# Two row tiles of a matmul one sum apart, released by a GpSimd token, with paced loads

## The chip, the cores and the metric

The kernel runs on one core of one Trainium2 chip. The metric is device time in microseconds (us). Runs are compared within the same rounds on the same chip; all runs compared here are in the fast state (the single look at one kernel has no state of its own and is marked). "Span" is the time from the first to the last instruction of the one profiled execution, some 1.7 to 2 us less than device time.

## The reference, cut to what matters

```python
# x: (8, 4096, 192); weight: (8 heads, 7); w_in: (192, 2048); w_out: (2048, 192); all float32
w = softmax(weight)                                   # per head
x_pad = concat([zeros(6 rows), x])                    # causal, per batch row
out = einsum('hk,bskhg->bshg', w, windows(x_pad, 7))  # a 7-tap convolution down the sequence
h = out.reshape(32768, 192) @ w_in
g = maximum(0.01 * h, h)
return g @ w_out
```

So: a depthwise convolution, a matmul up to 2048 columns, a leaky rectifier, a matmul down to 192.

## The kernel before

Two batch rows are worked on at once, 512 positions of each in a block; 32 blocks. The data of a block goes through these stages:

- GpSimd issues six loads of x with a cast to bf16 (`load_x`); SyncE (SP) issues three transposing DMAs (`transpose_x`), which lay the channels on the partitions.
- VectorE (DVE) does the convolution: 3 pieces of 64 channels, 7 instructions each.
- TensorE (PE) does the first matmul with two 64-row tiles side by side; ScalarE (ACT) takes the product out of PSUM (the memory, divided into banks, that TensorE writes to) through the rectifier.
- TensorE does the second matmul, also with two 64-row tiles. A "sum" is one output tile of 128 rows: 16 matmuls of row tile 0 and 16 of row tile 1, added into the same PSUM bank.

The first five blocks are cut into halves (ten groups of 256 positions), so that work can start early. Each group is a number of steps: two units of the first matmul, then a batch of slots of the second. In a slot row tile 0 does one matmul, and row tile 1 another one, `LAG` slots behind. The program must keep the two row tiles from writing one bank at the same time (the prediction names the page of the Trainium skill that says so). So row tile 1 starts a sum only after row tile 0 has finished it, and the order is kept by a dependency on an instruction of another engine:

```python
    LAG = NFC + NFC // 2          # 24 slots; a sum has NFC = 16
...
    def mm1(grp, u):
        ...                                       # the matmuls of one unit
        act = nc.scalar.activation(out=g[blk][...], in_=ph..., func=Prelu, alpha=0.01)
        while unsealed:
            seal[unsealed.pop()] = act.ins.name   # the release of finished sums

    def mm2_one(rt, m, fc):
        ins = nc.tensor.matmul(...)
        if rt == 0 and fc == NFC - 1:
            unsealed.append(m)
        if rt == 1 and fc == 0:
            tc.add_manual_dep(ins.ins, seal[m], ..., reason="other row tile, same bank")
...
        for j in range(steps):
            for u in range(2 * j, 2 * j + 2):
                mm1(grp, u)
            for _ in range(quota):
                mm2_slot(slot)                    # stores an output tile after every second sum
                slot += 1
            if i == 1 and j == 1:
                nc.gpsimd.tensor_copy(out=pjunk, in_=g[0][...])   # a gate: x waits for the weights
                load_x(2)
            if i == 2 and j == 1:
                transpose_x(2)
            for job in ahead[per * j : per * (j + 1)]:
                job()                             # convolution of the next group, on VectorE
            if j == steps // 4 and last_half:
                load_x(blk + 3)
            if j == steps // 2 and last_half and blk > 0:
                transpose_x(blk + 2)
```

## Time and profile before

| | before |
|---|---|
| median of 3 runs | 697.73 us (697.35 to 700.79) |
| span of the profiled run | 696.7 us |
| busy: TensorE, VectorE, ScalarE, GpSimd | 99%, 78%, 74%, 20% |
| opening (10 half groups), until the first full group | 117.5 us |
| one full block in the steady part | 20.96 us |

Two things are to be read here. The busy shares are means over the kernel. And a timeline line has the columns: start in us, length in us, engine, line, operation, output and input, shape, count, and in brackets the idle time of the engine before it, with what ended that. The lines themselves stand in the prediction.

### The profile page before, as it was taken

To read this page: it belongs to the slowest core of one execution; us is meant where nothing else is said; L and a number is where in the kernel's file an instruction comes from. 1 tells how busy PE (TensorE), PEld (TensorE's weight loads), DVE (VectorE), ACT (ScalarE), POOL (GpSimd) and SP (SyncE) were. 2 spreads that over 40 slices of the span, in tenths; PEclk is the share of its full clock that TensorE was granted. 3 is DMA by queue.
4 is the path that set the end of the run, shared out by engine and by line. 5 is a ranking of instruction groups with operands and counts; after the bars stand their busy time and mean duration, and the time that the engine had idled before them with its cause. 6 is when DMAs were issued, how large, how long until landed. Compare 5 with 4: busy or idle time off the path is not lost.

```text
span 696.7 us, 26003 instructions
## 1 busy us (share of the span) xinstructions
PE 688.9 (99%) x11756; PEld 611.7 (88%) x11756; DVE 542.4 (78%) x1000; ACT 512.3 (74%) x576; POOL 142.2 (20%) x199
## 2 busy tenths in 40 slices
PE   8999999999999999999999999999999999999997
PEld 6899998678888888888888888888888888888887
DVE  6899999867777787777787777787777787777712
ACT  6788887977777777777777777777777777777770
POOL 4732221320222220222211222220222210000000
PEclk9999999999999999999999999999999999999999
DMA  9987563754556545556644556544566535122112
GB/s 172 110 106 84 83 88 68 83 77 80 73 67 92 81 70 81 74 67 93 81 67 85 67 74 92 80 73 74 73 75 86 87 66 73 56 52 58 47 36 70
DMA packets 184847, 54.39 MB, mean 78 GB/s; under 512 B 148384, under 2 KB 184736, under 8 KB 184736
## 3 DMA queue, kind: packets, MB, share of 16 engines
q0 software_dynamic: 98768, 14.17, 29.4%
q1 hardware_dynamic: 85968, 38.56, 23.0%
q8 instruction: 92, 1.51, 0.9%
q14 instruction: 19, 0.16, 0.1%
HBM read 29.88 MB, written 25.17 MB: 79 GB/s over the span
## 4 chain that ended last, share of the span: by engine, by line
PE 83%; DVE 12%; DMA 3%; issue 1%; POOL 0%; ACT 0%; POOLq 0%; ACTq 0%
PE po L377 43%; PE ph L357 40%; DVE yt L182 11%; DMA w_out<-in_moe_w_out_dram 2%; DVE yt L176 1%; DMA w_in<-in_moe_w_in_dram 1%; POOL sel L228 0%; ACT g L364 0%; DVE xt L157 0%; POOL sel L226 0%; DVE o_sb L416 0%; POOL ident masks.py:199 0%; PE ptr L143 0%; POOL ident masks.py:197 0%; POOLq masks.py:199 0%
## 5 line engine op out<-in xcount | busy, mean ns | idle before, releaser
L364 ACT ACTIVATE g<-ph 128x1024 bf16<-128x1024 f32 x512 | 496.4, 1021 | 162.9 <-PE ph L357 162.9
L182 DVE SCALAR_TENSOR_TENSOR yt<-xt,wk,yt 128x512 bf16<-128x512 bf16 (+1 forms) x648 | 442.6, 683 | 17.6
L377 PE MATMUL po<-w_out,g 64*128 64x192 bf16 (+1 forms) x8048 | 398.2, 243 | 0.7 <-DMA w_out<-in_moe_w_out_dram 0.7
L377 PEld LDWEIGHTS <-g 64*128 64x128 bf16 (+1 forms) x8048 | 372.5, 94 | 29.4 <-issue 1.1
L357 PE MATMUL ph<-yt,w_in 64*128 64x512 bf16 (+1 forms) x3552 | 392.2, 347 | 2.3 <-ACT g L364 0.9
L357 PEld LDWEIGHTS <-w_in 64*128 64x128 bf16 x3552 | 250.1, 94 | 47.0 <-issue 5.3
L79 POOL DMA_DIRECT2D x_bf<-in_x_dram x180 | 133.6, 777 | 420.0 <-DMA xt<-x_bf 420.0
L416 DVE COPY o_sb<-po 128x192 f32<-128x192 f32 x216 | 77.3, 358 | 127.2 <-PE po L377 124.8
L176 DVE TENSOR_SCALAR yt<-xt,wk 128x512 bf16<-128x512 bf16 (+1 forms) x108 | 36.8, 340 | 0.2
L416 ACT COPY o_sb<-po 128x192 f32<-128x192 f32 x40 | 13.1, 327 | 0.0
L201 PE MATMUL acc<-xt,diag 64*64 64x256 bf16 x84 | 6.6, 319 | 0.0
L201 PEld LDWEIGHTS <-diag 64*64 64x64 bf16 x84 | 5.1, 126 | 1.4 <-issue 0.6
L250 PE MATMUL warm<-zero 128*128 128x256 bf16 x18 | 4.3, 399 | 1.1 <-DVE junk L218 1.1
L238 POOL DMA_DIRECT2D w_in<-in_moe_w_in_dram x8 | 5.1, 644 | 0.0
L157 DVE COPY xt<-ptr 128x384 bf16<-128x384 bf16 x7 | 2.2, 354 | 2.4 <-PE ptr L143 2.4
L250 PEld LDWEIGHTS <-zero 128*128 128x128 bf16 x18 | 2.0, 131 | 2.2 <-DVE junk L218 1.1
L296 ACT ACTIVATE diag<-ident,wkl 128x64 bf16<-128x64 bf16 x14 | 3.6, 336 | 0.0
L128 DVE CAST x_bf<-x_nat 128x384 bf16<-128x384 f32 x5 | 2.4, 499 | 1.4 <-DMA x_nat<-in_x_dram 1.4
L461 POOL COPY pjunk<-g 1x1 bf16<-1x1 bf16 x1 | 0.2, 177 | 12.0 <-ACT g L364 12.0
L128 ACT CAST x_bf<-x_nat 128x384 bf16<-128x384 f32 x3 | 1.5, 506 | 1.5 <-DMA x_nat<-in_x_dram 1.5
L317 ACT ACTIVATE yt<-acc,rsum 128x256 bf16<-128x256 f32 x2 | 0.9, 473 | 2.2 <-PE acc L201 2.2
L255 ACT ACT_TABLE_LOAD x1 | 1.3, 1283 | 0.8 <-PEq L498 0.8
(29 smaller groups left out, 13.7 us busy)
## 6 DMA issues: line engine op xcount, KB each, us to landing
out_dram<-o_sb SPq DMA_DIRECT2D x128, 192.0 KB, 2.1
x_bf<-in_x_dram POOLq DMA_DIRECT2D x180, 64.0 KB, 3.2
x_nat<-in_x_dram SPq DMA_DIRECT2D x8, 192.0 KB, 4.8
w_in<-in_moe_w_in_dram POOLq DMA_DIRECT2D x8, 192.0 KB, 8.7
xt<-x_bf SPq DMA_TRANSPOSE x90, 2.5
w_out<-in_moe_w_out_dram POOLq DMA_DIRECT2D x1, 768.0 KB, 14.7
w<-in_weight_dram SPq DMA_DIRECT2D x1, 0.2 KB
```

The lines of the kernel that those rows point to most:

```text
L79: nc.gpsimd.dma_start(out=t[:, c, :, e, :], in_=src[2 * rp + e, :, :, c * CH : (c + 1) * CH],)
L128: copy(out=x_bf[q // 2][:, :, h * HS : (h + 1) * HS, e, :], in_=x_nat[q][:, e, :, :].rearrange("p s (c k) -> p c s k", c=NCH),)
L176: lambda s=src, d=dst, c=c: nc.vector.tensor_scalar_mul(d, s, wk[:, c, 0:1])
L182: lambda s=src, d=dst, c=c, k=k: nc.vector.scalar_tensor_tensor(out=d, in0=s, scalar=wk[:, c, k : k + 1], in1=d, op0=mybir.AluOpType.mult, ...
L201: lambda k=k, p=p, a=a, e=e, ps=ps: nc.tensor.matmul(out=acc[ps, :T], lhsT=diag[c][ps, p, k, :], rhs=xt[0][ps, c, a : a + T], start=(k == ...
L238: nc.gpsimd.dma_start(out=w_in[e * CH : (e + 1) * CH, :, fs], in_=moe_w_in[:, fs].rearrange("(c p) f -> p c f", p=CH),)
L250: nc.tensor.matmul(out=wa[:, 0, 0:HT], lhsT=zero[:, 0:128], rhs=zero, start=True, stop=True)
L296: act = nc.scalar.activation(out=diag[c][:, 1, k, :], in_=ident2, func=mybir.ActivationFunctionType.Copy, scale=wkl[:, c, k : k + 1],)
L357: nc.tensor.matmul(out=ph[:, e, i * T : (i + 1) * T], lhsT=w_in[ps, c, f * 128 : (f + 1) * 128], rhs=y[ps, c, t0 : t0 + T], start=(c == 0) ...
L364: act = nc.scalar.activation(out=g[blk][:, nf * u : nf * (u + 1), :, t0 : t0 + T], in_=ph.rearrange("p e (i t) -> p i e t", i=nf), func=my ...
L377: ins = nc.tensor.matmul(out=po[m], lhsT=g[b][ps, fc, e, s * 128 : (s + 1) * 128], rhs=w_out[ps, fc, :], start=(rt != 1 and fc == 0), stop ...
L416: copy(out=o_sb[:, n % 2, :], in_=po.pop(n))
```

## The change

Its intent: shorten the lag to one sum, so that the end has fewer slots in which only one row tile works. Row tile 1 then needs its release at the very start of a batch, and the release comes from GpSimd: a one-element memset that follows the first matmul of the next step. Since GpSimd takes its queue in order, its loads must not hold the token up, so they are issued one in a step (two in the half groups). Three lines of the driver, which place loads and transposes, moved along with it.

```diff
-    LAG = NFC + NFC // 2
+    LAG = NFC
...
+                    if unsealed:                      # inside mm1, after its first matmul
+                        token = nc.gpsimd.memset(ptoken, 0.0)
+                        tc.add_manual_dep(token.ins, ins.ins.name, ..., reason="row tile 0 has left its bank")
+                        while unsealed:
+                            seal[unsealed.pop()] = token.ins.name
-        while unsealed:
-            seal[unsealed.pop()] = act.ins.name
...
-            if i == 2 and j == 1:
+            if i == 3 and j == 0:
                 transpose_x(2)
...
-            if j == steps // 4 and last_half:
+            if j == 0 and last_half:
                 load_x(blk + 3)               # now only puts six loads on a list
-            if j == steps // 2 and last_half and blk > 0:
+            if loads:
+                loads.pop(0)()
+            if loads and T < ST:
+                loads.pop(0)()
+            if j == steps - 2 and last_half and blk > 0:
                 transpose_x(blk + 2)
```

More of the change, by code (lines that the diff above doesn't have):

```diff
@@ L68 @@
     x_nat, x_bf, xt = {}, {}, {}
+    loads = []
     def load_x(blk):
@@ L78, in load_x @@
             for e in range(2):
-                nc.gpsimd.dma_start(
-                    out=t[:, c, :, e, :],
-                    in_=src[2 * rp + e, :, :, c * CH : (c + 1) * CH],
+                loads.append(
+                    lambda c=c, e=e: nc.gpsimd.dma_start(
+                        out=t[:, c, :, e, :],
+                        in_=src[2 * rp + e, :, :, c * CH : (c + 1) * CH],
+                    )
                 )
@@ L356, in mm1 @@
                     ps = slice(e * CH, (e + 1) * CH)
-                    nc.tensor.matmul(
+                    ins = nc.tensor.matmul(
                         out=ph[:, e, i * T : (i + 1) * T],
@@ L363, in mm1 @@
                     )
-        act = nc.scalar.activation(
+                    if unsealed:
+                        token = nc.gpsimd.memset(ptoken, 0.0)
+                        tc.add_manual_dep(
+                            token.ins, ins.ins.name,
+                            mybir.DependencyInfo(
+                                mybir.DependencyClass.Sync, mybir.DependencyReason.DATA
+                            ),
+                            reason="row tile 0 has left its bank",
+                        )
+                        while unsealed:
+                            seal[unsealed.pop()] = token.ins.name
+        nc.scalar.activation(
             out=g[blk][:, nf * u : nf * (u + 1), :, t0 : t0 + T],
@@ L424 @@
     pjunk = const_pool.tile([1, 1], BF16)
+    ptoken = const_pool.tile([1, 1], FP32)
     slot, avail = 0, 0
```

## The prediction

> **What bounds the kernel now.** I read the page first, then the chain of work that ended last in order of time, the waits, and the timeline around the places where that chain leaves TensorE. The page's busy line and its chain by engine:
>
> ```profile
> PE 688.9 (99%) x11756; PEld 611.7 (88%) x11756; DVE 542.4 (78%) x1000; ACT 512.3 (74%) x576; POOL 142.2 (20%) x199
> ...
> PE 83%; DVE 12%; DMA 3%; issue 1%; POOL 0%; ACT 0%; POOLq 0%; ACTq 0%
> ```
>
> TensorE (PE) looks like the only bound, but 12% of the chain is VectorE (DVE). The chain in order of time shows where: from the first token block (28.3 us) until 118.9 us it runs through the convolution on VectorE, without a break, and only then goes over to TensorE. The windows of those 90.6 us and of the long steady part:
>
> ```profile
> 28.30:118.90 90.60, 89.86 (x1908) 89.45 (x1904) 85.19 (x180) 73.33 (x103) 25.57 (x35) 1.00 0.70 86
> 140.00:660.00 520.00, 520.00 (x8738) 458.58 (x8734) 411.25 (x720) 384.66 (x398) 93.56 (x126) 1.00 0.50 74
> ```
>
> (Columns: window, length, busy PE, weight loads, DVE, ACT, POOL, then clock, DMA share, GB/s.) So there are two regimes. In the steady part PE is busy 520.00 of 520 and DVE 79%: PE bounds. In the opening part, ten groups of 256 rows, both are near full, and DVE sets the time: the timeline shows it arriving late at the first full group.
>
> ```profile
> 114.25 4.69 DVE L182 SCALAR_TENSOR_TENSOR yt<-xt,wk,yt 128x512 bf16<-128x512 bf16 x6
> ...
> 118.99 1.04 PE L357 MATMUL ph<-yt,w_in 64*128 64x512 bf16 x8 [0.83 <-DVE yt L182]
> ```
>
> The last convolution piece ends at about 118.94, and PE, idle for 0.83 us, goes on at 118.99. Any delay of VectorE between 28.3 and 118.9 moves the end of the kernel one for one. The place in that stretch which the change touches, from the timeline:
>
> ```profile
> 39.04 0.38 SPq L419 DMA_DIRECT2D out_dram<-o_sb  x1
> 39.53 4.57 SPq L94 DMA_TRANSPOSE xt<-x_bf  x3
> ...
> 43.55 0.28 DVE L176 TENSOR_SCALAR yt<-xt,wk 128x256 bf16<-128x256 bf16 x1
> 43.87 1.49 PE L357 MATMUL ph<-yt,w_in 64*128 64x256 bf16 x24
> ...
> 54.39 1.49 PE L357 MATMUL ph<-yt,w_in 64*128 64x256 bf16 x24
> ```
>
> The three transposes of block 2 start on the SyncE queue (SP) at 39.53 and are in by 44.10; VectorE reads the first of them at 43.55, with no idle time before it. PE wants the product of that convolution at 54.39.
>
> **What the Trainium skill says.** "PSUM — Partial Sum Buffer", section "PSUM bank collisions raise a hardware error", says that different row tiles may not write one PSUM bank at once and that software must order them; that is why row tile 1 needs a release at all. The trace shows no cost of this order now: among PE's waits none is for the second matmul's release. "Perfetto Trace Analysis", section "Tensor Engine Instruction", calls ACT, DVE and GpSimd strict FIFO, so a GpSimd token waits behind a load placed ahead of it; in this trace GpSimd waited 420.0 us in all at its loads, which would be fatal for a token. "GPSIMD Engine Reference", section "Specifications", says that GpSimd shares SBUF interfaces with VectorE. The trace agrees in part: one TENSOR_SCALAR of 128x256 at 46.88 took 0.54 us beside GpSimd's load issues, against 0.28 elsewhere, while the SCALAR_TENSOR_TENSORs kept their 0.50. "TensorE: Matmul & The Clock Gate", part 1, says that PE drops to half clock after an idle window of about 3.4 us; the trace before has no such idle stretch after the start (clock 1.00 in all windows).
>
> **The change part by part.**
> *Lag 24 to 16 slots.* A slot is one matmul of each row tile; from the timeline 16 slots take 1.32 us, 0.0825 each, also where only one row tile works. The number of slots is a constant plus the lag, so 8 fall away: 8 x 0.0825 = 0.66 us saved, at the end, where before 8 slots follow the last group. Otherwise it removes no PE time, as PE waits for nothing here now.
>
> *The token.* 247 memsets of one element (counted in the built program's order). A token follows the first matmul of a step, so it may run some 0.3 to 0.5 us into the step; its reader is the second weight load of the step's batch, at 1.29 us (timeline: 12 matmuls from 399.83, batch from 401.12). A memset of this kind took 0.10 us at the start of the trace. About 0.6 us of slack is left, so cost 0, if GpSimd is free. That is what the loads one a step are for: a load issue is 777 ns (745 to 879), it stands just after a token, and the next token comes 2.61 us later; with two a step (in the opening part) 1.55 us. Since each load is now requested after the transposes it depends on are long done, the 420 us of waiting should vanish. Cost 0.
>
> *Copies of the output move to the end of a step.* In a full block VectorE's step is then: copy at batch end + 0.28, three pieces to +2.88 (timeline: copy at 404.67, pieces to 407.27), as long as a PE step, 2.61. The last three pieces of a block fall in its last step and end 0.27 us into the next block, where PE wants them after two pairs of matmuls, 2 x 0.213 = 0.43. That fits by about 0.1 us. I allow 0.3 us in all for small misses over 21 blocks.
>
> *Loads of block 3 ahead of block 2, transposes of block 2 later.* This I expect to be the real cost. In the built order block 3's loads are now requested first (step 0 of the second group), then block 2's, so the transposes of block 2 go from step 1 of the third group to step 0 of the fourth; on SP four output stores stand ahead of them, before two. SP takes its queue in order; it waited 92.0 us in all for ACT's copies. The fourth store needs sum 7, whose row tile 1 now ends with the batch of that very step. From the trace: that batch ends at 46.50 (45.18 + 1.32); the copy starts 0.2 later (in the tail, batch end 679.57, copy at 679.77) and takes 0.33: 47.03; the store's issue until the transposes took 0.49 before (39.04 to 39.53): transposes at 47.5; one takes 2.5 us to land (page, part 6): 50.0, with the semaphore 50.1. VectorE would have started at 43.55: **6.55 us late.** Nothing else stands in its queue that it could do in between. PE then stalls about 5 us at 54.4 (third convolution piece at 50.1 + 3 x 3.32 = 60.1), and the rest, some 1.5 us, at the first full group, since PE's group takes 10.52 us and VectorE's 9.97. Everything after is PE bound again, so 6.55 us reach the end.
>
> *Early loads.* Two loads of block 3 are issued before the gate that kept x off the DMA engines until the weights are in. If they delay w_out (landing at 23.95, on the chain), all shifts. They stand behind it in the same queue, so I take 0.1 us, at most 2 (each load estimated at 1.06 us of all 16 engines: 29.4% of 16 x 697 us over 98,768 packets is 33 ns, by 512 packets, by 1/16).
>
> Sum: 697.7 - 0.66 + 6.55 + 0.3 + 0.1 = **704.0 us.**
>
> **Rivals.** (a) The opening delay does not occur: the transposes go early enough, or VectorE has slack. For it: the author chose the place on purpose, and VectorE's share looks moderate (78%). Against: the store ahead in SP's queue, and a chain through VectorE with no gap. It would give 697.1 to 697.5. (b) The token becomes the bound: GpSimd sits in a load or is held by VectorE, and each batch starts late; 0.2 us at each of 247 would be 49 us, 0.03 us 7 us. Against: 0.6 us of slack, load issues of at most 0.88 us. (c) VectorE's later copies make each full block late, by 0.1 to 0.3 us: 21 x 0.2 = 4 us more, 708. For it: the margin of only 0.1 us. Against: the page's idle time of VectorE before copies, 124.8 us, says it mostly waits for PE. (d) The 5 us stall cools PE's clock. It would cost some 1.7 us of PE time, but the later wait at the first full group (about 2.3 us) would hide it: 0.
>
> **Range and chances.** The main term rests on four measured durations and an order in the queue, so it is good to perhaps 1 us if the mechanism holds (85%). (a) takes 8%, (c) and early loads stretch the top. Range 700.5 to 708.0. Two per cent is 14 us; slower than that needs (b) or (c) in full, 5%; faster by 2% has no source, 1%; same 94%.
>
> **What would show it right or wrong.** In the changed profile: the first transpose of block 2 at about 47.5 after the fourth store; an idle stretch of VectorE of about 6.5 us before a TENSOR_SCALAR near 50; PE waiting for yt about 5 us near 54.5 and about 2.3 us near 124; the steady window still with PE at 100%, steps of 2.61 us, no PE wait for GpSimd; GpSimd's waits at transposes gone; the tail shorter by 0.66. Wrong if the transposes start before 45, if PE's waits for VectorE add up to under 3 us, or if the steady part's block differs from 20.96 us by over 0.1.

## The result, and the profile after

The changed kernel takes 705.45 us (median of 5 runs, 704.17 to 708.96), the kernel before in the same rounds 698.27 us. The ratio is 1.0106, with a 95% interval of 1.0073 to 1.0139. (A ratio here is the mean time of one kernel's runs over that of the other's runs of the same rounds, so it is not quite the ratio of the medians.) It is slower, by less than two per cent. The span went from 696.7 to 703.4 us.

The page of the changed kernel, its busy line and its chain by engine:

```profile
PE 689.6 (98%) x11756; PEld 550.0 (78%) x11756; DVE 549.1 (78%) x1000; ACT 516.5 (73%) x576; POOL 163.8 (23%) x446
...
PE 93%; DMA 3%; DVE 1%; ACT 1%; POOL 0%; issue 0%; SPq 0%; POOLq 0%
```

TensorE is busy for the same time as before, within 0.7 us, in a span 6.7 us longer: it idles more. VectorE has all but left the chain that ends last. The timeline of the changed kernel where block 2 is transposed, that is, the place that the prediction showed of the kernel before:

```profile
46.95 0.37 SPq L433 DMA_DIRECT2D out_dram<-o_sb  x1
47.44 3.94 SPq L98 DMA_TRANSPOSE xt<-x_bf  x3
51.40 0.29 DVE L180 TENSOR_SCALAR yt<-xt,wk 128x256 bf16<-128x256 bf16 x1 [8.40 <-DMA xt<-x_bf]
...
54.87 0.11 PEld L361 LDWEIGHTS <-w_in 64*128 64x128 bf16 x3 [0.65 <-DVE yt L186]
54.87 0.28 PE L361 MATMUL ph<-yt,w_in 64*128 64x256 bf16 x2 [0.43 <-ACT o_sb L430]
...
58.19 0.40 PE L361 MATMUL ph<-yt,w_in 64*128 64x256 bf16 x2 [3.03 <-DVE yt L186]
...
61.51 2.32 PE L361 MATMUL ph<-yt,w_in 64*128 64x256 bf16 x20 [2.92 <-DVE yt L186]
63.59 2.79 PE L391 MATMUL po<-w_out,g 64*128 64x192 bf16 x32
```

The fourth output store is issued at 46.95, the transposes follow at 47.44, and VectorE, idle for 8.40 us, gets the first at 51.40 instead of 43.55. TensorE then waits three times for the convolution, 6.4 us in all. (The first of the three matmul lines names ScalarE's copy instead, but that copy was over at 54.86, within 0.05 us of the convolution piece, 51.73 + 3.09 = 54.82; the weight load of the same moment names the convolution.) The last line shows an after-effect: a batch of 32 matmuls took 2.79 us, where it takes 1.50 elsewhere. The windows of that place and of the steady part (columns as in the prediction; the clock is the third number from the end):

```profile
62.00:68.00 6.00, 6.00 (x78) 5.55 (x76) 5.61 (x13) 2.92 (x4) 0.09 (x1) 0.58 0.06 19
68.00:74.00 6.00, 6.00 (x136) 6.00 (x132) 5.61 (x14) 5.25 (x8) 0.18 (x2) 1.00 0.16 49
143.69:687.63 543.94, 543.94 (x9141) 416.95 (x9136) 425.14 (x734) 404.12 (x419) 120.53 (x346) 1.00 0.50 75
```

The granted clock was 0.58 in the 6 us from 62 on, and 1.00 in the next 6. The last window holds the 26 full blocks after the first; the same blocks took, in the kernel before:

```profile
135.19:680.23 545.04, 545.04 (x9141) 479.88 (x9137) 416.92 (x732) 404.08 (x419) 96.95 (x131) 1.00 0.49 73
```

545.04 - 543.94 = 1.10 us less, over 26 blocks 0.042 us each. With that the whole difference can be added up. The lines at the two ends, first of the kernel before, then of the changed one:

```profile
135.19 1.58 PE L357 MATMUL ph<-yt,w_in 64*128 64x512 bf16 x12
678.91 14.13 PE L377 MATMUL po<-w_out,g 64*128 64x192 bf16 x168
...
143.69 1.48 PE L361 MATMUL ph<-yt,w_in 64*128 64x512 bf16 x12
686.31 13.47 PE L391 MATMUL po<-w_out,g 64*128 64x192 bf16 x160
```

| term | before | after | difference, us |
|---|---|---|---|
| first matmul of the second full group | 135.19 | 143.69 | +8.50 |
| the 26 full blocks | 545.04 | 543.94 | -1.10 |
| the last batch and the matmuls after it: 168 in 14.13 us, then 160 in 13.47 | 14.13 | 13.47 | -0.66 |
| sum | | | +6.74 |

(The last batch, 1.32 us in both kernels, also belongs to the last full block, so the rows overlap by it; the differences do not change.) The spans differ by 6.7 us, so nothing is left over. The 8.50 us fall in two. The last convolution piece for the first full group ended at 118.94 before (114.25 + 4.69) and at 126.34 after (121.65 + 4.69 in its timeline), 7.40 later. The other 1.10 are TensorE's: it reached that group only at 127.06, and did not wait there at all:

```profile
121.65 4.69 DVE L186 SCALAR_TENSOR_TENSOR yt<-xt,wk,yt 128x512 bf16<-128x512 bf16 x6
...
127.06 1.47 PE L361 MATMUL ph<-yt,w_in 64*128 64x512 bf16 x12
```

GpSimd, in the waits, no longer stands at its loads (420.0 us before) but at its tokens, as intended:

```profile
POOL ptoken L370 <- PE ph L361: 453.3, 247, 13.5
```

And no wait of TensorE for the token appears among its waits.

### The profile page after: what moved, and what is told of

Read it like the earlier page. It is cut to its first block, busy times and chain, and to the rows that moved or that the text cites. A ratio compares the mean times of both kernels' runs of the same rounds, so it can differ in the third digit from the quotient of the medians.

```text
span 703.4 us, 26493 instructions
## 1 busy us (share of the span) xinstructions
PE 689.6 (98%) x11756; PEld 550.0 (78%) x11756; DVE 549.1 (78%) x1000; ACT 516.5 (73%) x576; POOL 163.8 (23%) x446
## 4 chain that ended last, share of the span: by engine, by line
PE 93%; DMA 3%; DVE 1%; ACT 1%; POOL 0%; issue 0%; SPq 0%; POOLq 0%
PE po L391 48%; PE ph L361 45%; DMA w_out<-in_moe_w_out_dram 2%; DVE yt L186 1%; ACT g L380 1%; DMA w_in<-in_moe_w_in_dram 1%; DMA xt<-x_bf 1%; POOL sel L232 0%; DVE yt L180 0%; SPq L433 0%; POOL sel L230 0%; DVE o_sb L430 0%; ACT o_sb L430 0%; POOL ident masks.py:199 0%; POOL ident masks.py:197 0%
## 5 line engine op out<-in xcount | busy, mean ns | idle before, releaser
L391 PEld LDWEIGHTS <-g 64*128 64x128 bf16 (+1 forms) x8048 | 356.5, 94 | 45.4 <-issue 1.3
L361 PE MATMUL ph<-yt,w_in 64*128 64x512 bf16 (+1 forms) x3552 | 382.1, 348 | 8.0 <-DVE yt L186 6.0
L391 PE MATMUL po<-w_out,g 64*128 64x192 bf16 (+1 forms) x8048 | 386.6, 243 | 0.9 <-DMA w_out<-in_moe_w_out_dram 0.9
L361 PEld LDWEIGHTS <-w_in 64*128 64x128 bf16 x3552 | 193.2, 94 | 99.7 <-issue 10.0
L370 POOL MEMSET ptoken<- 1x1 f32 x247 | 21.8, 88 | 453.3 <-PE ph L361 453.3
L180 DVE TENSOR_SCALAR yt<-xt,wk 128x512 bf16<-128x512 bf16 (+1 forms) x108 | 43.4, 401 | 10.6 <-DMA xt<-x_bf 8.8
```

Source lines behind the costliest of these rows:

```text
L180: lambda s=src, d=dst, c=c: nc.vector.tensor_scalar_mul(d, s, wk[:, c, 0:1])
L361: ins = nc.tensor.matmul(out=ph[:, e, i * T : (i + 1) * T], lhsT=w_in[ps, c, f * 128 : (f + 1) * 128], rhs=y[ps, c, t0 : t0 + T], start=(c ...
L370: token = nc.gpsimd.memset(ptoken, 0.0)
L391: ins = nc.tensor.matmul(out=po[m], lhsT=g[b][ps, fc, e, s * 128 : (s + 1) * 128], rhs=w_out[ps, fc, :], start=(rt != 1 and fc == 0), stop ...
```

## The experiments

My theory: the loss is the late arrival of block 2's transposed data, and nothing else; shorter lag and token are a small gain. The main rival: the shorter lag or the token costs the time. Then there was one thing that the prediction did not have, the 1.10 us gained in the steady part.

### The order mended: block 2's loads first, its transposes where they were

```diff
 # against the changed kernel
                 nc.gpsimd.tensor_copy(out=pjunk, ...)
-                load_x(2)
-            if i == 3 and j == 0:
+            if i == 2 and j == 1:
                 transpose_x(2)
...
+            if i == 1 and j == 0:
+                load_x(2)
             if j == 0 and last_half:
                 load_x(blk + 3)
```

> The changed kernel with block 2's loads requested before block 3's and block 2's transposes back at step 1 of the third group; token, lag of 16 and one load a step stay. Theory (the loss is the late transposes of block 2, nothing else): VectorE has no idle stretch at 43 us, TensorE no 3 us waits for yt, clock 1.00 throughout, the steady part keeps its 20.92 us a block, and the kernel beats both: 696.1 us (698.3 - 0.66 tail - 1.1 steady - 0.4 earlier VectorE), at most 697.2. Rival (the short lag or the token costs the time, in the steady part or the opening): still 703 to 705.

Measured: 696.51 us (6 runs), before 698.56 (11 runs), ratio 0.9966, interval 0.9943 to 0.9989. VectorE has no idle stretch for a transpose; TensorE's one wait for the convolution is that at the first full group, shorter than before:

```profile
118.52 1.04 PE L361 MATMUL ph<-yt,w_in 64*128 64x512 bf16 x8 [0.60 <-DVE yt L186]
```

The rival falls: lag, token and paced loads are all still there, and 9 us are gone. This kernel beats both, by about a third of a per cent. Its span is 2.3 us below that of the kernel before: 1.10 of the steady part, 0.66 of the tail, and 0.47 because the first full group goes on at 118.52, not at 118.99.

### The late transposes alone

```diff
 # against the changed kernel
-    LAG = NFC
+    LAG = NFC + NFC // 2
 # and ScalarE's activation as the release again, as before the change
```

> The changed kernel with lag 24 and ScalarE's release as before; only the new order of the loads and the later transposes of block 2 are left. Theory: now three output stores, not four, stand ahead of the transposes, and the third is free at about 44.3 us, so the transposes start at 44.8, VectorE at 47.5 to 48.8, 4 to 5 us late against the kernel before: 702 to 703.5 us, steady block 20.96. It should lie between the two kernels: the late place alone costs most, the short lag adds the fourth store. Rival (the loss comes of lag and token): 698.3.

Measured: 703.38 us (4 runs), before 698.30, ratio 1.0073 (1.0056 to 1.0090). The transposes start at 46.06, later than the 44.8 I expected, and VectorE starts at 48.59, inside the expected stretch:

```profile
46.06 5.03 SPq L98 DMA_TRANSPOSE xt<-x_bf  x3
...
48.59 0.29 DVE L180 TENSOR_SCALAR yt<-xt,wk 128x256 bf16<-128x256 bf16 x1 [3.79 <-DMA xt<-x_bf]
...
58.70 1.80 PE L361 MATMUL ph<-yt,w_in 64*128 64x256 bf16 x20 [2.63 <-DVE yt L186]
60.27 2.68 PE L381 MATMUL po<-w_out,g 64*128 64x192 bf16 x32
```

The moved lines alone, without lag and token, make most of the loss: 5.1 us over the kernel before, where the changed kernel has 7.2. A single wait of 2.63 us was followed here by a slow batch (2.68 us); the granted clock in the window of that batch, 60.27 to 62.95, was 0.55.

### The transposes ahead of the fourth store

```diff
 # against the changed kernel
-            if i == 3 and j == 0:
+            if i == 2 and j == 3:
                 transpose_x(2)
```

> The changed kernel with the transposes of block 2 one step earlier, before the fourth store instead of behind it, its loads as they are. Theory: the transposes start at about 42.2 us, land at 44.7 to 45 beside no loads, VectorE idles 1.7 to 2 us, no long wait of TensorE, clock 1.00: 697.8 us (up to 699). If the landing of the loads, not the store, held the transposes: as the changed kernel, 705.

Measured: 697.29 us (4 runs), before 698.30, ratio 0.9983 (0.9966 to 0.9999). The loads stand as in the changed kernel, only the place in SP's queue is another, and the transposes start at 42.37:

```profile
42.37 3.93 SPq L98 DMA_TRANSPOSE xt<-x_bf  x3
...
44.91 0.29 DVE L180 TENSOR_SCALAR yt<-xt,wk 128x256 bf16<-128x256 bf16 x1 [1.69 <-DMA xt<-x_bf]
```

So it was the store ahead in the queue, which waited for ScalarE's copy, and not the loads' landing, that held the transposes until 47.4.

### No loads beside the transposes

```diff
 # against the changed kernel
-            if j == 0 and last_half:
+            if j == (2 if i == 3 else 0) and last_half:
                 load_x(blk + 3)
```

> The changed kernel with block 4's loads requested two steps later, so that none is in flight beside the transposes of block 2. Theory (the first transpose took 3.9 us to land, not 2.5, because loads shared the DMA engines): VectorE starts at 50.0 us, not 51.4, and the kernel takes 704.0 us, 1.4 less. Rival (a first transpose behind a store takes 3.9 us anyway): VectorE at 51.4, 705.4.

Measured: 704.09 us (4 runs), before 698.30, ratio 1.0082 (1.0067 to 1.0097).

```profile
47.26 3.92 SPq L98 DMA_TRANSPOSE xt<-x_bf  x3
...
49.80 0.29 DVE L180 TENSOR_SCALAR yt<-xt,wk 128x256 bf16<-128x256 bf16 x1 [6.97 <-DMA xt<-x_bf]
```

From issue to use 49.80 - 47.26 = 2.54 us, against 51.40 - 47.44 = 3.96 in the changed kernel. The two kernels before this one, in whose timelines GpSimd issues no load from the issue of the first transpose until it has landed, agree: 2.53 (late transposes alone) and 2.54 (ahead of the fourth store). The term that I had mis-sized is thereby found: not the place in the queue but the landing.

### The stall filled

```diff
 # against the changed kernel, in mm1 at i == 4, u == 0, before the 2nd and 3rd channel piece:
+                    for _ in range(24):
+                        nc.tensor.matmul(out=wf[:, 0, 0:HT], lhsT=zero[:, 0:128], rhs=zero, start=True, stop=True)
```

> The changed kernel with 24 throw-away matmuls (2.6 us) in each of TensorE's two waits for yt near 55 and 58 us, so that its clock does not drop. Theory (the cooled clock made TensorE later than VectorE at the first full group, 0.65 us): clock 1.00 between 60 and 80 us, TensorE waits for yt at the first full group again, 704.8 us, 0.65 less. If the cooled clock was hidden, as the prediction said: 705.4, no difference.

Measured: 704.55 us (4 runs, 703.46 to 708.86), before 698.30, ratio 1.0100 (1.0065 to 1.0134). By its time this run is inconclusive: its interval holds the changed kernel's 1.0106 too. Its profiled span, 701.4 us, is 2.0 below the changed kernel's, but 0.8 of that has nothing to do with the fill: VectorE had its first transposed data at 50.58, not 51.40. The trace is clear about the mechanism. The batch after the stall takes 1.50 us again, the clock is 1.00 in that stretch, and TensorE again arrives first at the first full group and waits:

```profile
60.68 1.27 PE L368 MATMUL ph<-yt,w_in 64*128 64x256 bf16 x20 [0.31 <-DVE yt L186]
61.77 1.50 PE L398 MATMUL po<-w_out,g 64*128 64x192 bf16 x32
...
123.58 0.61 PE L368 MATMUL ph<-yt,w_in 64*128 64x512 bf16 x4
125.54 1.04 PE L368 MATMUL ph<-yt,w_in 64*128 64x512 bf16 x8 [1.35 <-DVE yt L186]
```

From the end of the stall to the first full group TensorE took 123.58 - 60.68 = 62.90 us here and 127.06 - 61.51 = 65.55 in the changed kernel, over the same matmuls: the low clock cost 2.65 us. So it did reach the end of the changed kernel, by about the 1.1 us that TensorE was later than VectorE.

### Six loads in one step

```diff
 # against the mended kernel
+            while loads and T == ST:
+                loads.pop(0)()
```

> The mended kernel with all six loads of a full block issued in one step. Theory (GpSimd takes its queue in order, so the next token waits for six issues of 0.74 us and more): TensorE's batch in step 1 of each of the 24 blocks with loads starts about 1.6 us late: 696 + 24 x 1.6 = some 734 us. If GpSimd's queue did not hold the token up, or the token were not needed so early: within 1 us of the mended kernel.

Measured: 734.62 us (one look, its state unknown; the waits in its trace make up the difference). The waits of TensorE name the token:

```profile
PE po L391 <- POOL ptoken L370: 34.3, 23, 1.5
```

and one case in the timeline shows how: six issues take 4.45 us, the token, due at about 137.9, comes after them, and the batch stops after its first matmul.

```profile
135.85 4.45 POOL L82 DMA_DIRECT2D x_bf<-in_x_dram  x6 [0.51 <-issue]
...
140.23 0.10 POOL L370 MEMSET ptoken<- 1x1 f32 x1
140.39 1.49 PE L391 MATMUL po<-w_out,g 64*128 64x192 bf16 x31 [1.49 <-POOL ptoken L370]
```

The loads one a step are therefore not decoration: they are what makes this token on GpSimd free.

### Lag and release taken apart

Two kernels, both on the mended one: the long lag with the token, and the long lag with ScalarE's release.

```diff
-    LAG = NFC
+    LAG = NFC + NFC // 2
 # second kernel: also seal[...] = act.ins.name, no token
```

> The mended kernel with the lag of 24 slots again, still released by the token. Theory: the tail is 0.66 us longer than in the mended kernel, the steady block stays at 20.92 us (the token, not the lag, took the 0.04 us a block): 696.8 us. Rival (the short lag gave the shorter block): block 20.96 us, 697.9 us.

> As the run before, but the release is ScalarE's activation again, as in the kernel before; so this is the kernel before with its loads one a step. Theory: steady block 20.96 us again, 697.9 us, that is 1.1 us over the token with the same lag. Rival: the same as with the token (within 0.3 us), block 20.92.

Measured: 698.22 us with the token and 698.07 with ScalarE's release (6 runs each; ratios 0.9990, 0.9968 to 1.0013, and 0.9986, 0.9966 to 1.0006). The expected 1.1 us does not show in the times. The traces show it in the steady part, 544.04 us for the 26 blocks with the token and 545.04 without; but the token's kernel lost some of it in the opening, where VectorE waited 0.51 us for a transpose and TensorE 1.37 us at the first full group: its second full group starts at 135.22 us, the other's at 134.96. That leaves 0.7 us between the two profiled spans (695.7 and 696.4); but the profiled run is the fastest of the six with the token, and why the other five are slower is not shown. With the long lag the second output store comes later (at 38.58 us, against 36.35 in the mended kernel), and block 2's transposes wait behind it. Since that disturbs the comparison, I repeated it with the transposes one more step earlier (`i == 2 and j == 0`), in three kernels.

> The mended kernel with the transposes of block 2 one more step earlier, so that no kernel of this set waits for them: lag 16, token. Theory: VectorE waits for no transpose; as the mended kernel, 696.3 us, block 20.92 us.

> The same with the lag of 24 slots. The earlier comparison of the two releases with this lag was spoilt: the token's kernel waited 0.5 us for a transpose in the opening. Theory (the lag is worth its tail alone): 0.66 us more than with the short lag, 696.9 us, block 20.92 us.

> The same with the lag of 24 and ScalarE's release. Theory (the activation that released the row tile ends just too late in the first step of every block): the first batch of each block 0.04 us longer, block 20.96 us, 26 x 0.042 = 1.1 us more than with the token: 698.0 us. Rival (the token only moves the wait elsewhere): within 0.3 us of the token's kernel.

| kernel | median of 6, us | lowest to highest | 26 blocks, us | ratio to before (698.50) |
|---|---|---|---|---|
| short lag, token | 696.25 | 695.93 to 697.33 | 543.94 | 0.9962 (0.9943 to 0.9980) |
| long lag, token | 696.60 | 696.45 to 696.83 | 544.04 | 0.9965 (0.9945 to 0.9985) |
| long lag, ScalarE | 698.38 | 697.28 to 700.80 | 545.04 | 0.9993 (0.9971 to 1.0014) |

Now the release shows in the times too: all six runs with ScalarE's release are slower than all six with the token at the same lag, by 1.8 us in the medians, of which the steady part explains 1.00. One run of the last kernel, its slowest and the profiled one, has a mean clock of 0.997; its trace has a wait of 2.29 us for w_out, and slow matmuls after it. Without that run the median of the other five is 697.89, 1.3 us over the token. The lag itself is worth 0.35 us in the medians. Its two tails are the 13.47 and 14.13 us of the changed kernel and the kernel before, but in the profiled runs the short lag's second full group starts 0.52 us later (134.85 against 134.33), which takes most of that back.

Two more things stand in these traces. The kernels with ScalarE's release hold all the moved lines and still take 545.04 us for the 26 blocks, as the kernel before did: the moved lines neither cost nor gain anything there. And the list of loads does not space the loads by itself: without the token GpSimd again issues six in one go (in the first long-lag kernel with ScalarE's release from 198.79 on, for 4.45 us). It is the tokens between them, each waiting for TensorE, that space them.

Where the 0.04 us a block lies is seen in the timeline of the kernel before, at the first step of a block:

```profile
302.87 1.53 PE L357 MATMUL ph<-yt,w_in 64*128 64x512 bf16 x12
303.86 1.94 ACT L364 ACTIVATE g<-ph 128x1024 bf16<-128x1024 f32 x2 [0.74 <-PE ph L357]
304.17 1.60 PE L377 MATMUL po<-w_out,g 64*128 64x192 bf16 x32
305.53 1.53 PE L357 MATMUL ph<-yt,w_in 64*128 64x512 bf16 x12
...
306.45 1.94 ACT L364 ACTIVATE g<-ph 128x1024 bf16<-128x1024 f32 x2 [0.66 <-PE ph L357]
```

The activation that releases row tile 1 starts 0.99 us into this step (303.86 - 302.87), against 0.92 in the next (306.45 - 305.53). It takes 1.02 us, so it ends at about 304.88; row tile 1 wants it in the middle of the batch, at 304.17 + 8 x 0.0825 = 304.83. The batch lasts 1.36 us until the next step, not 1.32. The token of the changed kernel starts 0.50 us into a step and is over at 0.59, 0.7 us ahead of the batch (327.33 against 328.04 in its timeline). Why ScalarE starts later there is argued from the built program only: the first activation of a block waits for one more semaphore, because it writes a new buffer.

## Why the prediction was right

The time, 705.45 us, lies in the range, 1.45 over the 704.0 that the sum gave, and the mechanism was the one named as the real cost. By its own steps:

- **Later transposes of block 2: right in mechanism, short in size.** The transposes were to start at 47.5 and started at 47.44; four stores stood ahead. The term that was off is the landing: taken as 2.5 us from the page's median, it was 3.96, because the loads of block 4, which the change itself places there, were in flight (the run without them: 2.54). So VectorE was 7.85 us late (51.40 against 43.55), not 6.55; by the first full group 7.40 of it were left, as the chain from the first piece to the last took 74.94 us instead of 75.39.
- **The stall "cools PE's clock ... would hide it: 0": wrong.** The cooling came, and I put its cost at 1.7 us against some 2.3 us of cover. It cost 2.65 us (by the filled stall), and the cover, TensorE's wait at the first full group of the filled kernel, was 1.35: TensorE's own waits before it had been longer than the 5 us that I expected, 6.4. Of the 1.30 us between cost and cover 1.10 is seen at the end (the other 0.2 is not accounted for), and the wait of 2.3 us that I named as a sign did not come. The filled stall showed it in the trace, though not clearly in the time.
- **Lag: right.** 8 slots, 0.66 us, exactly.
- **Token cost 0: right. That "the trace shows no cost of this order now", and that the lag "removes no PE time" elsewhere: wrong.** There was a cost, below what the list of waits resolves: 0.04 us in every block. A block of 20.96 us is 0.08 more than 8 steps of 2.61 (half of that is rounding: the changed kernel's block is still 20.92), and I did not ask why; the first step was 2.66 us long (302.87 to 305.53). The term for "small misses" in the full blocks, +0.3, measured -1.10. (There are 27 full blocks, not the 21 that I counted.)
- **Copies at the end of a step: right.** The margin of 0.1 us held; the full blocks have TensorE busy throughout.
- **Early loads: right.** w_out let TensorE start at 23.86, 0.13 earlier than before. (The wait for w_out is 0.4 to 2.3 us over the profiled kernels that list one, so 0.13 says little.)

In sum: 6.55 + 0.3 + 0.1 - 0.66 = 6.29 was predicted, and 7.40 + 1.10 - 1.10 - 0.66 = 6.74 was measured in the traces. Rival (b), a token held up by loads, is real, but only when the loads are bunched (34.3 us). Of rivals (a) and (c) nothing was seen. That the sums lie so close is in part luck: VectorE's lateness and the clock came out 0.85 and 1.10 us above their terms, the full blocks and the early loads 1.40 and 0.10 below theirs. One reading was too clean: the clock of the kernel before was 1.00 in every window of 20 us but the last, where it was 0.93.

## What to carry to other kernels

An engine with a mean of 78% can be the bound of a stage, as VectorE was in the opening here: look for where the chain of work leaves the busiest engine, and treat every delay there as a delay of the whole. When a DMA is moved in a program, look at its place in the queue of its issuing engine as well as at the readiness of its data: here a store ahead, which waited for a copy of that very step, held up the transposes behind it. And let a release between engines rest on the earliest event that proves the point and on an engine whose queue is kept short; here one slightly longer step in eight was the sign of a release that came just too late.

## What the Trainium skill lacked or had wrong

- "TensorE: Matmul & The Clock Gate", part 1, puts the drop of the clock after an idle window of about 3.4 us (it also tells of a kernel whose short gaps made the clock swing, but not how long they were). Here single waits of 2.63 and 2.29 us were followed by matmuls at about half speed (a batch of 2.68 us instead of 1.50; granted clock 0.55 and 0.52 in the slow stretches), and waits of 1.35 us were not.
- "DMA: Bandwidth & Descriptors" has no figure for how a transposing DMA fares beside loads. Here the first of three was usable after 2.53 to 2.54 us alone and after 3.96 with GpSimd's loads in flight. The median over all 90 transposes was 2.5 us in the four kernels without the token and 2.9 to 3.2 in the nine with it, the one with six loads in one step included; what makes that difference is not shown.
- No page that I read gives the price of a release between engines through a one-element memset on GpSimd: 0.50 us from the start of the step to its start, 0.09 us long, and no wait of TensorE for it where the batch that reads it starts 0.7 us after its end. What such a token costs behind six load issues is 1.49 us each time.
